# Another hand-written order of 1489 tasks for a fused long convolution and state-space scan

## The chip, the core and the metric

The kernel runs on one core of one Trainium2 chip. The metric is the device time of one execution in microseconds (us). The core has five instruction queues that run in parallel, each in its own order: TensorE (PE in the profile, its weight loads PEld), VectorE (DVE), ScalarE (ACT), GpSimd (POOL) and SyncE (SP). In this kernel SP and POOL do little but issue DMA transfers: SP's go through the queue that the profile calls q1, POOL's through q0.

## The reference, cut to what matters

Two layers work on sequences of 2048 steps and 1024 channels, and their outputs stand side by side:

```
# A: short causal filter of k, gate with v, long convolution over time, gate with q
k_shift = sum over t in 0..3 of k_pad[:, t:t+S, :] * shift_k[:, 3-t]
kv  = k_shift * v
y   = irfft(rfft(kv, 2S) * rfft(ssm_k, 2S))[:S] + kv * ssm_D
a   = q * y
# B: complex diagonal state-space layer, 1024 states
Bu  = x @ B_bar.T                     # complex
h_t = Lam_bar * h_(t-1) + Bu_t        # 2048 steps
b   = 2 * Re(h @ C.T) + x * Dskip
out = concatenate([a, b], axis=-1)
```

Tensors are bf16.

## The kernel before, in words

Both layers are cut into tasks, and one string, `ORDER`, names all 1489 of them in the order in which their instructions are issued. A word of it is `task.arguments:slots`. The letters of the slots say where a result lies: `a` is a place in `arena` (53 units of 1024 bf16 columns), `p` one of the eight PSUM banks, `h` one of three state buffers (`gslot`), `w` one of three weight slots (`wslot`). Each task goes to its own engine, every engine runs its tasks in the order of the string, and the framework sets the semaphores between them from the buffers that they read and write. So the string decides three things at once: the order on each engine's queue, which buffer must come free first, and, through the name of the task, which engine does a copy or issues a transfer.

**Layer B, sixteen chunks of 128 steps.** `bl` (L420) loads blocks of B, `bT` (L415) transposes them on PE and `bc` (L431, on ACT; `bcv` on DVE) copies them into `BT`; `cl`, `cT` and `cc`, or `cx`, do the same for C. `x.i` (L447) loads chunk i of x with a transposing DMA on SP's queue. `U.i.jp.jl` multiplies it with `BT` (L464, 16 matmuls of 128x128), `ue` (L473) copies the result out of PSUM on ACT, and `uev` does so on DVE. `r1` and `r2` (L487, L498, DVE) rotate, `cy` (L500, ACT) carries the state over, `sc` (L504, DVE) is the scan, `r3` and `r4` (L487, L510, DVE) rotate back. `yq` (L538, quarter matmuls of 64x64, eight pieces to a chunk) or `y` (L520, L523) multiplies with C, `ye` (L556) copies it out. Stores of the output are `yst` and `ysg` on POOL's queue (L563), `ysp` and `ysh` on SP's (L564).

**Layer A, two-step transforms.** `ld_w` loads the filter taps, `wb` (L402) spreads them over the partitions by a matmul with a row of ones, and `wbe` copies them out. `kp.r` (L570, and L572 with L573 for the two earlier blocks) loads blocks of k into a ring, `vp` loads v. `kvm`, `kva`, `kvb` and `kvc` (L587 to L602, DVE) build kv. `am` (L607) is the first transform, `ae` (L613) copies it out, and `ast` (L616, POOL) stores it in DRAM as `Ys_kv`; `hl`, `hd`, `hT`, `hc`, `hm`, `he` and `hst` do it for the filter, into `Ys_h`. `hd` adds `ssm_D`, on ACT, or as `hdv` on DVE.

The second transform goes over sixteen pairs. For pair i, `lw.i` (L671, SP) loads 160 KB of weights into one of the three weight slots; `lh.i` and `lk.i` (L676, SP) load 512 KB each of `Ys_h` and `Ys_kv`. For each half g = 2i, 2i+1 of the pair, `sh.g` and `sk.g` (L687, PE) transform them, and `she` (L696) and `ske` (L703) copy the results out. Two `sw.i` copies (L707) swap even and odd rows by DMA, one for each half of the rows, on POOL's queue (`sw`) or on SP's (`swp`). `pr.i` (L713, DVE) multiplies, `sa.g` (L725, PE) transforms back, `sae` (L733) copies out, `vst.i` (L736, POOL) stores 512 KB in `Vs`. The weight slot is free when the pair's last `sa` is done.

The last stage loads `vl` (L741) and q (`qp`, L746) on SP, `a3` (L753, PE) is the last transform, `a3e` (L760) copies out, `qm` (L762, DVE) multiplies with q, and `ost` (L763, POOL) or `osp` (L764, SP) stores.

A copy out of PSUM has the name of its task for ACT (`she`, `ske`, `sae`, `a3e`, `ue`, `ye`), and the name with a `v` behind it for DVE.

Setting up: `ld_par` loads five rows of parameters (L273, SP), `par_T` (L279) transposes them on PE, and `p32` (L284) copies the result out on DVE; tables are made from them.

Of the kernel before, what the change touches and what calls it, by code (L numbers as in the profile page):

```python
# [72 lines left out]
ue.1.0:a34 bl.3.1:a19 bc.4.0 U.0.0.0:p5 U.0.0.1 bl.7.0:a41 bT.2.1:p4 bl.6.1:a12 U.0.2.0:p0 bT.3.1:p7 bc.5.0 U.0.2.1
bT.7.0:p6 stt ue.0.0:a24 bl.7.1:a20 bc.2.0 bc.2.1 x.2:a52 bT.6.1:p2 bT.7.1:p3 cl.1.0:a15 kp.-2 bT.3.0:p4 bc.7.0 kring
bc.3.1 x.3:a21 bc.3.0 U.1.2.1:p5 bc.7.1 U.1.2.0 cl.1.1:a37 U.1.1.1:p1 bc.6.1 U.1.1.0 cl.3.1:a14 U.0.3.1:p4 ue.0.2 ue.1.2
kvm.1:a16 z2 kvm.2:a42 U.0.3.0 rta kva.1 kva.2 z1 U.0.1.0:p7 kvb.1:a39 cT.1.0:p6 U.3.0.1:p3 ue.0.3 kvb.2:a12 U.0.1.1
ue.0.1 cc.1.0 cT.3.1:p0 vp.1:a27 kvm.0:a16 cl.0.1:a48 kvb.3:a26 kva.0 kvc.3 cc.3.1 ld_Q ue.1.1 vp.0:a40 kvb.0:a36
# [5 lines left out]
ae.0.0.1 ast.0 am.1.0:p2p7 ae.1.0.1:a45 U.2.2.1 cx.6.1 r2.3:h2 ast.3 hT.0.1:p4 r1.1:a27 hT.0.6:p3 ae.1.1.0 U.2.3.1:p7
kvm.4:a14 ae.1.1.1 ue.2.2 cx.4.1 ae.1.0.0 r2.1:h0 hd.0 am.2.0:p6p5 hc.0.1:a22 U.2.3.0 ae.2.1.0 ast.1 cx.7.1 hd.1 ue.2.3
cT.2.0:p1 ae.2.0.0 hT.0.3:p2 cc.2.0 hc.0.6:a32 U.2.1.0:p7 U.2.1.1 hc.0.3:a13 hT.0.7:p0 hm.0.6.1:p4p1 hT.0.4:p6 cx.4.0
cy.1 kva.4 y.0.0.0:p3 ue.2.1 ast.2 sc.1.1 hc.0.4:a28 sc.1.0 hc.0.7:a12 y.0.0.1 hm.0.4.0:p2p6 kvb.4:a31 he.0.6.1.0:a43
he.0.4.0.1:a29 he.0.4.0.0 he.0.6.1.1 hT.0.0:p5 cx.5.0 hT.0.5:p0 vp.2:a34 y.0.0.2 hT.0.2:p1 r3.1:a45 hc.0.0:a19
hm.0.6.0:p6p2 he.0.6.0.0 hm.0.4.1:p5p4 he.0.4.1.1 he.0.4.1.0 y.0.0.3 hst.0.6.1 y.0.1.0:p6 kp.3 ye.0.0:a25 hc.0.5:a14
kvc.4 hst.0.4.1 y.0.1.1 he.0.6.0.1 r4.1 y.0.1.2 hm.0.0.1:p0p5 hc.0.2:a20 hm.0.7.0:p4p7 he.0.7.0.1:a50 y.0.1.3 r1.2:a15
hst.0.4.0 he.0.0.1.1:a48 hm.0.0.0:p2p3 hm.0.5.1:p7p5 y.1.1.0:p1 hst.0.6.0 he.0.7.0.0 kvm.6:a38 he.0.0.1.0 he.0.0.0.1  # L90
y.1.1.1 he.0.5.1.0:a23 he.0.0.0.0 hm.0.5.0:p4p2 he.0.5.1.1 he.0.5.0.1 vp.3:a26 am.4.0:p0p7 ye.0.1 he.0.5.0.0
ae.4.1.0:a29 x.4:a32 kp.4 y.1.1.2 y.1.1.3 y.1.0.0:p6 r2.2:h1 ae.4.0.0 kva.6 hm.0.7.1:p0p3 ye.1.1:a28 hst.0.7.0
hm.0.3.0:p2p5 hm.0.3.1:p7p4 y.1.0.1 kvm.5:a14 he.0.7.1.0 ysp.0 he.0.7.1.1 am.4.1:p1p0 cy.2 kvb.6:a19 kva.5 kvc.6
he.0.3.1.1:a36 y.1.0.2 he.0.3.1.0 kvb.5:a25 hst.0.0.1 he.0.3.0.0 hm.0.1.0:p3p2 hl.2.0:a44 sc.2.1 hst.0.5.1 hl.2.1
ae.4.0.1 U.4.3.1:p7 U.4.3.0 he.0.3.0.1 ae.4.1.1 he.0.1.0.1:a38 U.4.0.0:p2 kvc.5 hst.0.5.0 kvm.7:a13 hst.0.0.0 he.0.1.0.0
ue.4.3:a23 am.6.1:p4p7 ae.6.1.1:a17 am.6.0:p1p3 sc.2.0 hst.0.7.1 y.1.0.3 U.4.0.1 hst.0.3.1 ae.6.0.1 ae.6.1.0 ae.6.0.0
ye.1.0 hm.0.1.1:p3p1 hd.2 hm.0.2.1:p7p4 kva.7 he.0.1.1.0 he.0.1.1.1 hm.0.2.0:p0p6 he.0.2.0.1:a34 ast.6 he.0.2.1.1
hst.0.3.0 he.0.2.0.0 U.4.1.1:p5 U.4.1.0 hl.3.1:a40 r3.2:a48 ue.4.1 kvb.7:a31 hl.3.0 hT.1.4:p3 hc.1.4:a19 hT.1.5:p0
hT.1.6:p6 hst.0.1.1 hT.1.2:p4 he.0.2.1.0 hc.1.6:a22 U.4.2.1:p1 r4.2 hc.1.5:a33 hst.0.2.0 hc.1.2:a17 kvc.7 hst.0.2.1
hst.0.1.0 cy.3 ue.4.0 ast.4 hT.1.3:p5 am.5.1:p7p3 U.4.2.0 ue.4.2 y.2.0.0:p6 am.5.0:p2p0 sc.3.1 hT.1.7:p4 ae.5.0.1:a15  # L100
x.6:a37 lw.1:w2 hc.1.3:a18 y.2.0.1 ae.5.1.0 y.2.0.2 sc.3.0 hT.1.1:p1 hc.1.7:a35 hm.1.7.1:p4p5 y.2.1.0:p7 hd.3 ae.5.0.0
ae.5.1.1 am.7.0:p0p2 he.1.7.1.1:a25 hT.1.0:p5 y.2.1.1 hc.1.1:a14 ae.7.1.0:a38 kvm.8:a48 x.5:a36 ae.7.0.0 r3.3:a42
# [739 lines left out]
```

## Time and profile before

| what | value |
| --- | --- |
| median of the runs shown | 350.45 us (348.97 to 351.01) |
| the profiled execution | 352.94 us, of which the span from first to last instruction is 351.0 |
| mean granted clock of TensorE | 0.989 of full speed |
| busy: PE, DVE, ACT, POOL | 332.9, 326.1, 273.4, 68.0 us |
| DMA | 62880 packets, 101.09 MB, mean 288 GB/s |
| SP's queue (q1), POOL's queue (q0) | 67.39 MB, 32.95 MB |

The profile is of one execution. Its page gives busy times, the span in 40 slices, the queues, the chain of work that ended last and the costliest groups of instructions; the trace behind it can be asked for any stretch, any line and every wait. In a row of single instructions the first number is the start in us and the second how long it took; what stands in square brackets is the wait ahead of it and what ended it. A row of an issuing queue (SPq, POOL) gives the issue of a transfer, not its passing.

### The profile page before, as it was taken

The numbers are of one execution on the slowest core, as the hardware profiler recorded it, in microseconds if no ns is written. First come the engines' busy times: TensorE is split into PE (matmuls) and PEld (weight loads), VectorE is DVE, ScalarE is ACT, GpSimd is POOL, SyncE is SP. The second block draws the span as 40 slices with busy tenths as digits, with TensorE's granted clock in tenths as the row PEclk, the third lists the DMA queues.
The fourth block names the chain that finished last, engine by engine and source line by source line (L and its number), as shares of the span: only waits on it lengthen the run. The fifth ranks groups of instructions, "written<-read, shape, count | busy, mean of one in ns | idle before, by whom it ended". The sixth has DMA issues, their size and how long they took to land. (4 is left out here: it accounts for less than half of the span.)

```text
span 351.0 us, 11815 instructions
## 1 busy us (share of the span) xinstructions
PE 332.9 (95%) x5105; PEld 233.2 (66%) x5105; DVE 326.1 (93%) x261; ACT 273.4 (78%) x524; POOL 68.0 (19%) x110
## 2 busy tenths in 40 slices
PE   5989999999999999999999989999699999999991
PEld 2789888547856886689665565765575887754440
DVE  4999999999999999999999989999779999999961
ACT  6999999999999973798889769999378974235640
POOL 6000011343422552120111210031021122000020
PEclk9999999999999999999999999999899999999997
DMA  5999999898996888968998999898978898798996
GB/s 193 357 286 293 278 264 324 271 288 329 279 327 211 319 283 234 324 233 307 308 244 293 194 357 357 309 236 250 292 264 301 288 314 310 229 381 273 366 326 226
DMA packets 62880, 101.09 MB, mean 288 GB/s; under 512 B 29422, under 2 KB 31742, under 8 KB 62828
## 3 DMA queue, kind: packets, MB, share of 16 engines
q1 hardware_dynamic: 53228, 67.39, 66.1%
q0 software_dynamic: 9600, 32.95, 25.9%
q8 instruction: 40, 0.66, 0.8%
q14 instruction: 12, 0.10, 0.1%
HBM read 52.08 MB, written 33.55 MB: 244 GB/s over the span
## 5 line engine op out<-in xcount | busy, mean ns | idle before, releaser
L464 PEld LDWEIGHTS <-BT 128*128 128x128 bf16 x2048 | 118.4, 99 | 13.7 <-issue 9.2
L464 PE MATMUL bank<-arena,BT 128*128 128x128 bf16 x2048 | 126.0, 221 | 0.3 <-ACT BT L431 0.3
L538 PE MATMUL bank<-CT,gslot 64*64 64x512 bf16 x1408 | 88.2, 378 | 0.1
L504 DVE TENSOR_TENSOR_SCAN gslot<-rtab,gslot 128x1040 bf16<-128x1040 f32 x32 | 72.9, 2310 | 0.7
L538 PEld LDWEIGHTS <-gslot 64*64 64x64 bf16 x1408 | 38.8, 107 | 29.4 <-issue 1.4
L473 ACT CAST arena<-bank 128x512 bf16<-128x512 f32 x61 | 37.2, 642 | 14.0 <-PE bank L464 13.0
L613 ACT CAST arena<-bank 128x512 bf16<-128x512 f32 x64 | 36.6, 658 | 8.0 <-PE bank L607 5.3
L520 PE MATMUL bank<-CT,gslot 128*128 128x512 bf16 x160 | 39.4, 379 | 0.0
L696 ACT CAST arena<-bank 128x512 bf16<-128x512 f32 x62 | 33.4, 615 | 7.3 <-PE bank L687 5.7
L713 DVE TENSOR_TENSOR arena<-arena 128x4096 bf16<-128x4096 bf16 x16 | 36.5, 2285 | 2.3 <-ACT arena L473 1.6
L487 DVE TENSOR_TENSOR arena<-gslot,Z 128x4096 bf16<-128x4096 bf16 x16 | 36.6, 2288 | 0.9 <-PE bank L687 0.4
L703 ACT CAST arena<-bank 128x512 bf16<-128x512 f32 x60 | 33.7, 609 | 4.0 <-PE bank L687 2.6
L487 DVE TENSOR_TENSOR arena<-arena,Z 128x4096 bf16<-128x4096 bf16 x16 | 36.5, 2283 | 0.0
L733 ACT CAST arena<-bank 128x512 bf16<-128x512 f32 x60 | 32.7, 615 | 4.4 <-PE bank L725 4.4
L664 ACT CAST arena<-bank 128x512 bf16<-128x512 f32 x64 | 34.6, 635 | 1.7 <-PE bank L656 1.6
L587 DVE TENSOR_TENSOR arena<-arena 128x4096 bf16<-128x4096 bf16 (+3 forms) x16 | 29.9, 1880 | 0.0
L667 POOL DMA_DIRECT2D Ys_h<-arena x32 | 23.5, 737 | 28.6 <-ACT arena L664 26.1
L616 POOL DMA_DIRECT2D Ys_kv<-arena x16 | 11.1, 711 | 87.2 <-ACT arena L613 86.1
L687 PE MATMUL bank<-arena,wslot 64*64 64x512 bf16 x256 | 22.1, 383 | 4.7 <-DMA wslot<-a_c_W 4.7
L556 ACT CAST arena<-bank 128x512 bf16<-128x512 f32 x31 | 18.3, 601 | 9.9 <-PE bank L523 4.4
L760 ACT CAST arena<-bank 128x512 bf16<-128x512 f32 x26 | 13.6, 600 | 15.6 <-PE bank L753 15.6
L520 PEld LDWEIGHTS <-gslot 128*128 128x128 bf16 x160 | 14.4, 98 | 16.1 <-issue 1.5
(104 smaller groups left out, 416.8 us busy)
## 6 DMA issues: line engine op xcount, KB each, us to landing
Ys_kv<-arena POOLq DMA_DIRECT2D x16, 512.0 KB, 5.0
Ys_h<-arena POOLq DMA_DIRECT2D x32, 256.0 KB, 4.7
arena<-Ys_h SPq DMA_DIRECT2D x16, 512.0 KB, 7.2
arena<-Ys_kv SPq DMA_DIRECT2D x16, 512.0 KB, 5.4
Vs<-arena POOLq DMA_DIRECT2D x16, 512.0 KB, 5.7
arena<-Vs SPq DMA_DIRECT2D x16, 512.0 KB, 7.5
arena<-in_A_k_dram SPq DMA_DIRECT2D x8, 512.0 KB, 6.3
arena<-in_A_v_dram SPq DMA_DIRECT2D x8, 512.0 KB, 4.7
```

The source lines that it names most:

```text
L464: nc.tensor.matmul(pu[:, w, jl, :], BT[:, 2 * jp + jl, w, d, :], xT[:, d, :], start=(d == 0), stop=(d == ND - 1))
L473: cp(st["u", i][:, :, 2 * jp:2 * jp + 2, :], st.pop(("pu", i, jp)))
L487: nc.vector.tensor_mul(m, s_, win(Z))
L504: nc.vector.tensor_tensor_scan(gf, rtab[:].rearrange("p j t -> p (j t)"), gf, 0.0, ALU.mult, ALU.add)
L520: nc.tensor.matmul(py, h[:, w, j, 2:GW], CT[:, j, w, dh * 512:(dh + 1) * 512], start=(j == 0 and w == 0), stop=False)
L538: mm = nc.tensor.matmul(st["py", i, dh][cols, cs(r)], lhs(dh, rows, c), rhs(dh, rows), start=first, stop=last)
L613: cp(st["ysb", n2][:, p, dh * 512:(dh + 1) * 512], st.pop(("pa", n2, p, dh)))
L664: cp(o, st.pop(("pb", hf, s, e, r)).rearrange("p (n c t) -> p n c t", n=2, c=2))
L696: cp(st["hab", i][:, 0, a, l, :], st.pop(("ps", "h", g, l)))
L703: cp(st["x16", i][:, a, l, :], st.pop(("ps", "k", g, l)))
L713: nc.vector.tensor_mul(hab, st.pop(("x16", i)).rearrange("p a l d -> p (a l d)").unsqueeze(1).to_broadcast([P, 2, 2 * D]), hab)
L733: cp(st["vsb", i][:, a, dh * 512:(dh + 1) * 512], st.pop(("pv", g, dh)))
```

## The change

Only the text of `ORDER` differs. The 1489 tasks are the same but for the variants that name an engine or a queue. Of the copies out of PSUM, DVE does 23 instead of 20 and ACT three fewer (L760: 9 instead of 6; `shev` 4 instead of 2, `yev` 2 instead of 1, `saev` 3 instead of 4, `skev` 3 instead of 4, `uev` 2 instead of 3); `hd.0` becomes `hdv.0`. Some row swaps and some output stores change queues, so that SP's order has 138 rows instead of 136. Nearly every line of the string is another one; the lines that the prediction speaks of are these:

```diff
 ORDER = """
-ld_w:a15 wb.0:p2 ld_par wbe.0:a8 par_T:p7 p32 exp1 bl.6.0:a13 dve2 dve3 bl.0.0:a0 bl.0.1:a32 bl.1.0:a22 wb.4:p0
...
-bT.0.1:p2 sin0 bc.0.0 kp.1:a0 wb.1:p6 tabA1:a46a49a42a44 wb.6:p7 bc.0.1 wb.5:p3 kp.0 bT.1.0:p1 wbe.1 bl.5.1:a23 sin1
...
-bT.5.1:p6 bc.1.0 x.0:a38 bl.3.0:a48 bcv.6.0 eo kvm.3:a29 kp.-1 bT.1.1:p5 bT.4.0:p0 bcv.1.1 bcv.4.1 bc.5.1 kva.3 U.1.0.1
...
-yq.6.0:p7p6 ye.5.0:a11 vst.1 lk.2:a21 sh.5:p4p0 cy.7 sae.6.1 ye.5.1 yq.6.1 sh.4:p2p1 sae.6.0 she.4.1:a32 yq.6.2 yq.6.3
-she.4.0 sc.7.0 she.5.1 sk.5:p0p5 sc.7.1 r3.7:a45 sa.0:p1p3 r4.7 lh.4:a50 she.5.0 sa.1:p4p2 ske.5.1:a4 ske.5.0
...
-ske.11.1:a4 sae.5.0:a44 sk.10:p4p6 yq.7.4 yq.7.5 lk.4:a28 yq.7.6 lk.6:a21 lh.7:a12 swp.5.0 ske.10.1 sa.4:p3p6 x.11:a14
...
-yq.8.0:p1p0 yq.8.1 lw.6:w2 sh.13:p3p6 yq.8.2 lh.8:a37 lh.11:a1 sh.12:p2p5 r1.9:a40 she.13.0:a27 she.13.1 vst.2 lw.8:w1
...
-yq.10.0:p0p2 yq.10.1 ye.9.1 pr.9 sk.23:p3p4 yst.7 yq.10.2 ske.23.1 ske.23.0 sa.15:p5p1 yq.10.3 x.12:a52 sa.14:p7p3
-lw.10:w0 sae.15.1:a24 sae.15.0 sae.14.0 sa.18:p6p1 sa.19:p5p4 cy.11:h0 yq.10.4 ld_G sae.19.1:a49 sae.18.0 sw.11.0
...
-ye.10.0:a42 ye.10.1 shev.21.0:a5 she.20.1 lw.15:w2 lh.12:a1 she.21.1 U.12.1.0 sw.11.1 pr.11 ue.12.1:a22 sc.11.0
...
+ld_w:a41 wb.6:p6 wb.2:p5 wb.1:p0 wbe.1:a8 wbe.2 kp.0:a0 ld_par par_T:p1 wb.3:p7 wb.7:p4 p32 wb.0:p5 wbe.7 dd bl.2.1:a40
...
+bc.1.1 bT.0.1:p2 sin2 kva.1 bT.4.1:p0 bl.7.0:a40 kp.1 bT.5.0:p1 bc.4.1 bl.6.0:a39 bl.5.1:a43 bT.7.0:p7 x.0:a29 kp.-2
...
+bc.0.0 bc.5.1 U.1.1.0:p2 eo U.1.0.0 ue.1.0:a41 kvm.3:a35 cl.1.0:a19 U.0.2.1:p4 U.0.2.0 kvm.2:a13 U.1.2.0:p1 bc.6.0
...
+U.8.3.0:p4 r4.6 U.8.3.1 sae.3.0 cy.7 ye.5.1 pr.0 sa.7:p6p5 ue.8.3 sa.6:p1p0 sae.7.0:a38 sa.1:p3p7 vst.1 sa.0:p2p4
+sae.7.1 lh.4:a23 yq.6.0:p5p6 lh.2:a49 yq.6.1 sc.7.0 sae.1.1:a25 sae.6.0 sae.1.0 lw.2:w2 sae.0.1 lh.5:a32 r1.8:a42
...
+lk.7:a42 yq.7.5 ske.9.0 sa.11:p3p7 vst.3 r3.8:a36 sa.10:p6p0 sae.11.0:a12 sae.11.1 ske.9.1 sw.4.1 lw.6:w2 sae.10.0
...
+ske.12.1 x.11:a19 U.10.1.1 lw.8:w0 ue.10.1 lk.8:a25 sh.16:p0p3 ske.13.1 yq.8.4 ld_G swp.6.0 sk.17:p7p2 lw.7:w1
...
+she.18.1 x.12:a31 lh.12:a50 she.19.1 r2.10 sc.10.0 sc.10.1 r3.10:a7 r4.10 yst.8 sk.18:p2p4 pr.7 U.11.1.1:p6 U.11.1.0
...
+ske.22.1 lk.12:a6 sae.19.1:a33 sc.11.1 r3.11:a39 sae.18.0 U.12.0.1:p5 lw.10:w1 sh.20:p6p0 ye.10.0:a49 sae.19.0 lk.15:a8
...
+U.12.1.1 ske.21.1 vst.7 cy.12:h0 ske.20.1 uev.12.1 sa.22:p0p7 ue.12.2 sa.23:p2p6 sae.22.1:a38 sae.23.1 sae.23.0 lw.15:w2
+saev.22.0 sh.30:p3p5 shev.30.1:a44 r1.12:a34 sk.30:p1p4 x.13:a10 ske.30.0:a24 yq.11.0:p7p0 yq.11.1 sh.31:p1p2 skev.30.1
...
```

The place of `sa.0` and `sa.1` (PE) against `yq.6.0` is seen in these lines: before, eight PE tasks from `yq.6.0` to `sa.0` stand ahead of `sa.1`; now `sa.7`, `sa.6`, `sa.1` and `sa.0` stand ahead of `yq.6.0`. At three other places the queues read as follows.

SP's queue around the weight slot of pair 6 (in both pieces the L671 row that fills `wslot2`). L447 is the transposing load `x.11`, L676 the 512 KB loads, L707 the swaps, L671 the weight slots. Before:

```order
L676 DMA arena_95<-Ys_h_87 128x2x1024
L707 DMA arena_95<-arena_95 64x2048
L447 DMA_TRANSPOSE arena_95<-in_B_x_dram 128x8x128
L676 DMA arena_95<-Ys_h_87 128x2x1024
L707 DMA arena_95<-arena_95 64x2048
L671 DMA wslot2_94<-a_c_W3 128x640
L676 DMA arena_95<-Ys_h_87 128x2x1024 x2
L671 DMA wslot1_93<-a_c_W3 128x640
```

Now:

```order
L707 DMA arena_95<-arena_95 64x2048 x3
L676 DMA arena_95<-Ys_kv_86 128x2x1024
L671 DMA wslot2_94<-a_c_W3 128x640
L676 DMA arena_95<-Ys_kv_86 128x2x1024
L676 DMA arena_95<-Ys_h_87 128x2x1024 x2
L447 DMA_TRANSPOSE arena_95<-in_B_x_dram 128x8x128
L671 DMA wslot0_92<-a_c_W3 128x640
```

The slot of pair 6 was three transfers behind `x.11` and is now four ahead of it; what follows `x.11` directly now is the slot of pair 8.

SP's queue around the weight slots of pairs 10 and 15. Before, `x.12` (the L447 row), then the slot of pair 10, then that of pair 15:

```order
L671 DMA wslot1_93<-a_c_W3 128x640
L676 DMA arena_95<-Ys_h_87 128x2x1024 x3
L447 DMA_TRANSPOSE arena_95<-in_B_x_dram 128x8x128
L671 DMA wslot0_92<-a_c_W3 128x640
L671 DMA wslot2_94<-a_c_W3 128x640
L676 DMA arena_95<-Ys_h_87 128x2x1024
```

Now, from `x.12` to `x.13`; the slots of pairs 10 and 15 are the two L671 rows:

```order
L447 DMA_TRANSPOSE arena_95<-in_B_x_dram 128x8x128
L676 DMA arena_95<-Ys_h_87 128x2x1024
L676 DMA arena_95<-Ys_kv_86 128x2x1024 x2
L707 DMA arena_95<-arena_95 64x2048
L676 DMA arena_95<-Ys_h_87 128x2x1024
L707 DMA arena_95<-arena_95 64x2048
L676 DMA arena_95<-Ys_kv_86 128x2x1024
L671 DMA wslot1_93<-a_c_W3 128x640
L676 DMA arena_95<-Ys_kv_86 128x2x1024
L676 DMA arena_95<-Ys_h_87 128x2x1024
L671 DMA wslot2_94<-a_c_W3 128x640
L447 DMA_TRANSPOSE arena_95<-in_B_x_dram 128x8x128
```

Seven transfers stand now between `x.12` and the slot of pair 10, and `x.13` comes behind both slots.

The start of PE's queue: L402 are the `wb` matmuls that spread the filter taps, L279 is `par_T`. Before:

```order
L402 LDWEIGHTS ones_68
L402 MATMUL bank2_98<-arena_95,ones_68 128x512
L279 LDWEIGHTS praw_108
L279 MATMUL bank7_103<-ident_61,praw_108 128x40
L402 LDWEIGHTS ones_68
L402 MATMUL bank0_96<-arena_95,ones_68 128x512
```

Now:

```order
L402 LDWEIGHTS ones_68
L402 MATMUL bank6_102<-arena_95,ones_68 128x512
L402 LDWEIGHTS ones_68
L402 MATMUL bank5_101<-arena_95,ones_68 128x512
L402 LDWEIGHTS ones_68
L402 MATMUL bank0_96<-arena_95,ones_68 128x512
L279 LDWEIGHTS praw_113
L279 MATMUL bank1_97<-ident_61,praw_113 128x40
```

The parameter transpose came after one `wb` and comes now after three; on SP's queue its five loads stand now behind one 512 KB block of k (`kp.0`).

More of the change, by code (lines that the diff above doesn't have):

```diff
@@ L73 @@
[L73 to L77, printed above, removed]
@@ L83 @@
[L83 to L87, printed above, removed]
@@ L88 @@
[L88 to L102, printed above, removed]
@@ new lines @@
+r2.2 am.6.1:p0p4 ae.5.0.0 ae.6.1.0:a22 y.1.1.1 y.1.1.2 ae.6.0.1 kvm.7:a13 sc.2.0 hl.2.0:a44 kva.7 ae.6.1.1 sc.2.1
+kvb.7:a28 ue.4.3:a24 r3.2:a13 hm.0.1.1:p6p1 hl.2.1 hst.0.4.0 ae.6.0.0 hst.0.4.1 he.0.1.1.0:a38 hm.0.0.1:p2p0
+hm.0.0.0:p6p7 he.0.1.1.1 he.0.0.0.1:a48 y.1.1.3 hl.3.0:a40 hl.3.1 U.4.1.0:p4 U.4.1.1 he.0.0.1.0 ye.1.1 hst.0.1.1
+hm.0.1.0:p1p2 he.0.0.1.1 he.0.0.0.0 U.4.2.1:p6 ue.4.1 he.0.1.0.0 am.4.0:p0p5 ae.4.1.0:a30 ae.4.0.0 hd.2 ast.6 kvc.7
+U.4.0.1:p3 hst.0.0.1 U.4.2.0 hd.3 he.0.1.0.1 kp.4 ue.4.2 hT.1.3:p1 hc.1.3:a51 U.4.0.0 hst.0.0.0 hT.1.0:p7 hT.1.5:p0
```

185 lines of the change are left out of this document (102 added, 83 removed).

## The prediction

> **What bounds the kernel now.** I read the page first, then busy time over long stretches, then who waited for what, and then short windows around the longest waits.
>
> The page gives each engine's busy time, its share of the span and its instructions.
>
> ```profile
> PE 332.9 (95%) x5105; PEld 233.2 (66%) x5105; DVE 326.1 (93%) x261; ACT 273.4 (78%) x524; POOL 68.0 (19%) x110
> ```
>
> Two engines are nearly full, so 18 us on TensorE (PE) and 25 us on VectorE (DVE) are all that an order can win. Where most of it lies is seen in two long stretches (length, then busy us of each engine, granted clock, DMA share, GB/s):
>
> ```profile
> 45.00:180.00 135.00, 135.00 (x1966) 97.09 (x1967) 134.89 (x98) 117.54 (x228) 37.79 (x54) 1.00 0.91 282
> 180.00:260.00 80.00, 75.12 (x1420) 48.85 (x1412) 74.43 (x39) 64.61 (x132) 13.39 (x22) 0.98 0.97 282
> ```
>
> From 45 to 180 us neither engine has a gap: whatever makes either late there is still late at 180. From 180 to 260 both lose 5 to 6 us. The waits name the cause (total, times, longest):
>
> ```profile
> PE bank L687 <- DMA wslot<-a_c_W: 4.7, 3, 3.2
> DVE arena L696 <- PE bank L687: 2.5, 1, 2.5
> DVE arena L473 <- PE bank L464: 2.1, 1, 2.1
> DVE arena L713 <- ACT arena L473: 1.6, 1, 1.6
> ```
>
> PE waits for one kind of load, the 160 KB weight slots of the second transform; DVE's 2.5 and 2.1 are waits for that PE. Here are the two places, PE first, then the queues that issued what it waited for:
>
> ```profile
> 210.41 0.41 PE L687 MATMUL bank<-arena,wslot 64*64 64x512 bf16 x4 [1.32 <-DMA wslot<-a_c_W]
> 250.74 0.63 PE L687 MATMUL bank<-arena,wslot 64*64 64x512 bf16 x8 [3.19 <-DMA wslot<-a_c_W]
> ...
> 193.41 1.98 SPq L447 DMA_TRANSPOSE arena<-in_B_x_dram  x1
> 198.83 0.34 SPq L671 DMA_DIRECT2D wslot<-a_c_W  x1
> 240.78 1.27 SPq L447 DMA_TRANSPOSE arena<-in_B_x_dram  x1
> 243.02 1.32 SPq L671 DMA_DIRECT2D wslot<-a_c_W  x2
> ...
> 193.15 0.53 POOL L707 DMA_DIRECT2D arena<-arena  x1 [6.72 <-ACT gslot L500]
> 193.68 0.56 POOL L563 DMA_DIRECT2D out_dram<-arena  x1
> 241.45 0.56 POOL L563 DMA_DIRECT2D out_dram<-arena  x1 [3.08 <-ACT arena L556]
> 242.00 0.53 POOL L707 DMA_DIRECT2D arena<-arena  x1
> ```
>
> A weight slot issued at 198.83 is used at 210.41, and one issued at 243.02 at 250.74. Both stand behind a transposing load of x (L447) on SP's queue, and within 1.3 us of each of these loads POOL's queue issued at least two transfers. The two queues then nearly stop:
>
> ```profile
> 190.00:193.00 3.00, 3.00 (x76) 1.65 (x64) 2.74 (x2) 2.68 (x7) 0.00 (x0) 1.00 1.04 395
> 198.00:200.00 2.00, 1.88 (x43) 0.90 (x36) 2.00 (x2) 0.00 (x0) 0.00 (x0) 1.00 0.38 36
> 246.00:248.00 2.00, 1.55 (x36) 0.90 (x28) 1.90 (x2) 0.96 (x3) 0.00 (x0) 1.00 0.99 112
> ```
>
> The rate falls from 395 GB/s to 36 and 112. For contrast, the load issued at 227.90 has no POOL issue until 233.87, and the weight slot behind it (230.33) caused no wait above:
>
> ```profile
> 227.90 1.30 SPq L447 DMA_TRANSPOSE arena<-in_B_x_dram  x1
> 230.33 0.86 SPq L671 DMA_DIRECT2D wslot<-a_c_W  x1
> 233.87 0.73 POOL L736 DMA_DIRECT2D Vs<-arena  x1 [8.43 <-ACT arena L696]
> ```
>
> So my reading is that a transposing load that passes while POOL's transfers pass holds everything behind it on SP for about 5 us.
>
> **The change, part by part.** All sums are against the profiled execution, 352.94 us with a span of 351.0; the median of the runs shown is 350.45, or 2.5 less, and I carry the difference over unchanged.
>
> *The two holes.* In the new SP order the first slot load stands four entries ahead of the transposing load instead of three behind it. At the second place seven entries, two of them swaps that wait for late work, stand between the transposing load and the slot that followed it directly, and the next transposing load comes after both slots instead of before them. That takes PE's waits of 1.32 and 3.19, and the slow clock behind the second:
>
> ```profile
> 205.20 1.96 PE L464 MATMUL bank<-arena,BT 128*128 128x128 bf16 x32
> 251.30 3.58 PE L464 MATMUL bank<-arena,BT 128*128 128x128 bf16 x32
> 252.00:255.00 3.00, 3.00 (x32) 2.77 (x33) 3.00 (x2) 0.57 (x3) 0.00 (x0) 0.54 0.86 315
> ```
>
> The same 32 matmuls take 1.96 us at full clock and 3.58 after the wait, when the granted clock is 0.54: 1.62. Together 1.32 + 3.19 + 1.62 = 6.1 us on PE; on DVE 2.5 + 2.1 + 1.6 = 6.2.
>
> Would the new positions make holes of their own? Behind the first transposing load now stands the slot of pair 8, with 8.9 us of PE work between its release and its first use, more than the 7.7 that the slot at 243.02 took through a hole. Behind the slot of pair 15, the transposing load is followed, by the PE work between, about 3 us later by two 512 KB stores of `Vs` on POOL. If that meeting costs the same 5 us, it delays the swaps of pair 10 and one 512 KB load, wanted more than 8 us later; the next slot (pair 12) is issued some 9 us of PE work later. So nothing for either in the sum; if a cover fails it costs one hole, 3.19 + 1.62 = 4.8.
>
> *PE is now held to DVE at one place.* In the old order PE does four pieces `yq.6.0` to `yq.6.3`, `sh.5`, `sh.4`, `sk.5` and `sa.0` before `sa.1`; the new order puts `sa.1` ahead of all eight, and what DVE does ahead of `pr.0` is the same but for the small terms below. `sa.0` and `sa.1` read what `pr.0` writes.
>
> ```profile
> 179.56 2.29 DVE L713 TENSOR_TENSOR arena<-arena 128x4096 bf16<-128x4096 bf16 x1
> 180.41 0.84 PE L538 MATMUL bank<-CT,gslot 64*64 64x512 bf16 x12
> 184.76 1.06 PE L725 MATMUL bank<-arena,wslot 64*64 64x512 bf16 x16
> ```
>
> The first of the eight began at 180.41, so PE arrives at `sa.1` at 180.4 now, while `pr.0` (the DVE row) ended at 179.56 + 2.29 = 181.85. That is a wait of 1.4 us, plus whatever DVE itself is late. From the rows of the start:
>
> ```profile
> 3.67 0.58 PE L402 MATMUL bank<-arena,ones 1*128 1x512 bf16 x1 [3.67 <-DMA arena<-in_A_shift_k_dram]
> 4.18 0.21 PE L279 MATMUL bank<-ident,praw 40*128 40x40 bf16 x1
> 4.33 1.88 PE L402 MATMUL bank<-arena,ones 1*128 1x512 bf16 x4
> 4.43 0.20 DVE L284 CAST p<-bank 128x40 f32<-128x40 bf16 x1 [3.43 <-PE bank L279]
> ```
>
> DVE's first real work waits for the parameter transpose (L279), which stood behind one broadcast matmul and now stands behind three, at a pitch of (1.88 - 0.58) / 3 = 0.43: it starts at 3.67 + 3 x 0.43 = 4.96 instead of 4.18, so DVE is 0.78 late. The five parameter loads also stand behind a 512 KB load now; they have until 4.9 to land, so I add nothing (at worst one such load's time, 512 KB at 395 GB/s = 1.3 us). PE's wait at `sa.1` comes to 1.4 + 0.8 = 2.2 us. It is paid once: later places where PE now follows `pr` closely find it already that late. Bounds: 0 if PE arrives late by small waits of its own, 3.5 with the 1.3.
>
> *Copies between engines.* Evictions done by DVE go from 20 to 23, and one tiny add moves from ScalarE to DVE.
>
> ```profile
> L760 DVE CAST arena<-bank 128x512 bf16<-128x512 f32 x6 | 4.0, 687 | 0.5 <-PE bank L753 0.4
> ```
>
> Three at 0.687 make 2.1 us of DVE; the add (no row; DVE's small operations are near 0.2) is below the rounding. ScalarE, 78% busy, gains nothing by losing them.
>
> *Tighter loads.* Two later weight slots have 4.5 and 4.2 us of PE work between the release of their slot and their first use, and the `Vs` load that the last stage needs first is now fourth in its burst. What such a slot takes:
>
> ```profile
> wslot<-a_c_W SPq DMA_DIRECT2D x16, 160.0 KB, 3.3
> DMA to landing us min/median/max: 3.3/5.7/8.1
> ```
>
> (the first row is the whole run's median, the second the seven slots issued from 190 to 252, holes included). At 3.3 they fit, at 5.7 they cost 1.2 and 1.5. I take 1.0 in all, bounds 0 and 3.
>
> *The end* keeps its shape: last matmuls, one eviction, one store by each queue; 0.
>
> The sum on PE: -6.1 + 2.2 + 1.0 = -2.9. On DVE: -6.2 + 0.8 + 2.1 = -3.3, with some of the 1.0 on top. Both engines end within a microsecond of each other, so I take -3.0: 349.9 for the profiled execution, 347.4 for the median.
>
> [...]
>
> **The rivals.**
>
> *Full gain.* PE is late enough by itself at `sa.1` and all loads fit: DVE's -3.3 is the floor of that part, and the wait near the end goes too:
>
> ```profile
> DVE arena L762 <- DMA arena<-in_A_q_dram: 2.8, 1, 2.8
> ```
>
> In the new order the last loads of q have 7 us or more of work to land in. -3.3 - 2.8 = -6.1: 344.3. Against it: this asks every tight place to hold.
>
> *A hole moves.* The meeting named above, or one of another load, delays something wanted at once; one hole of 4.8 comes back: 347.4 + 4.8 = 352.2, or 350 where half is covered. For it: five transposing loads must still pass among POOL's stores. I put it at 351.
>
> *The holes are not made by the meeting.* If the stalls come from the mere number of transfers in flight, they return wherever the queues are as full: nothing won, 2.2 + 1.0 lost, 350.45 + 3.2 = 353.7, slower. For it: SP's queue was eight transfers deep at both. Against: the undisturbed load at 227.90. [...]
>
> *DVE loses at the start.* Its product `kvm.3` needs a block of k (`kp.1`), now behind fifteen other loads instead of eight.
>
> ```profile
> 0.00:10.00 10.00, 5.97 (x26) 2.48 (x27) 5.01 (x16) 6.97 (x12) 5.63 (x17) 1.00 0.68 195
> 10.00:20.00 10.00, 9.49 (x124) 9.16 (x124) 9.62 (x25) 9.90 (x24) 0.00 (x0) 1.00 1.08 362
> ```
>
> With itself these are three blocks of 512 KB and thirteen of 256 KB, 5.0 MB; 1.95 MB pass in the first 10 us and the rest at 362 GB/s in 8.4, so it lands near 18.4. DVE reaches it near 20.7 us (5.2, and some 15.5 of work ahead by the groups' means). Each microsecond beyond that is one lost, as 45 to 180 shows no slack; from 24 on the gain is gone, and at 27 the time is 350.45 + 3.3 = 353.7. Against it: the pace would have to fall by a third or more.
>
> **How the numbers follow.** Chances: forecast 0.50 (own range 345.5 to 349), full gain 0.14, a hole moves 0.16, not the meeting 0.12, late start 0.08. A measurement here tells no change from about 0.5%, which is 1.75 us: below 348.7 is faster, above 352.2 slower. Faster: nine tenths of the forecast and the full gain, 0.45 + 0.14 = 0.59. Slower: a fifth of the moved hole and the last two, 0.03 + 0.12 + 0.07 = 0.22. The same: 0.19. The range, 344.0 to 353.0, runs from the full gain to most of the moved hole and leaves out about 1 in 10 at each end.
>
> **What would show it.** Right: no wait of L687 for a weight slot above 1 us, the granted clock at full from 200 to 330, no window under 120 GB/s while slot loads wait, a PE wait near 2 us at 180 to 183 at L725, DVE's first copy near 5.2. Wrong: holes with no transposing load in them (the meeting is then not the cause), a wait of DVE at L587 before 25 us, or many small PE waits for ScalarE's evictions, whose cost I put at nothing because ScalarE is 78% busy.

## The result: 0.6% slower by the ratio, against a forecast of 0.9% faster

| | median of the executions shown | lowest to highest | profiled execution, its span |
| --- | --- | --- | --- |
| before | 350.62 us (20) | 347.00 to 353.26 | 352.94, 351.0 |
| changed | 351.35 us (20) | 350.12 to 353.66 | 353.08, 351.3 |

The ratio of changed to before is 1.0056, with a 95% interval of 1.0033 to 1.0080. It leaves out executions more than 1.5% above the fastest of their kernel, which takes four of the twenty from the kernel before and none from the changed one, so it is larger than the quotient of these medians, 1.002. The forecast was 347.4 with a range of 344.0 to 353.0: the time lies inside the range, but the gain of 3 us is not there; by the ratio the change loses 2.0 us, by the medians 0.7.

The page of the changed kernel, its first part:

```profile
PE 330.2 (94%) x5085; PEld 234.4 (67%) x5105; DVE 327.7 (93%) x265; ACT 272.4 (78%) x519; POOL 70.1 (20%) x113
```

DVE is busy 1.6 us longer than before (326.1); the rest is nearly the same. The long stretches tell more (length, then busy us of PE, PEld, DVE, ACT and POOL, granted clock, DMA share, GB/s). The changed kernel:

```profile
0.00:20.00 20.00, 12.42 (x105) 8.55 (x105) 13.03 (x31) 14.28 (x21) 5.11 (x16) 1.00 0.90 267
20.00:45.00 25.00, 23.58 (x407) 22.84 (x406) 24.76 (x41) 25.00 (x45) 0.00 (x0) 1.00 1.16 291
45.00:180.00 135.00, 133.13 (x1913) 95.83 (x1926) 134.64 (x98) 116.94 (x222) 38.66 (x56) 1.00 0.89 276
180.00:260.00 80.00, 79.25 (x1537) 55.50 (x1537) 77.41 (x43) 70.29 (x143) 13.31 (x21) 1.00 0.97 301
260.00:300.00 40.00, 38.05 (x694) 28.63 (x687) 34.45 (x25) 27.55 (x55) 7.95 (x12) 1.00 0.87 293
```

and the kernel before, where the prediction had not shown them:

```profile
0.00:20.00 20.00, 15.46 (x148) 11.64 (x149) 14.64 (x39) 16.86 (x35) 5.63 (x17) 1.00 0.88 279
20.00:45.00 25.00, 24.03 (x403) 22.65 (x401) 25.00 (x34) 25.00 (x35) 0.00 (x0) 1.00 1.17 289
260.00:300.00 40.00, 40.00 (x746) 30.41 (x743) 37.12 (x26) 29.58 (x60) 7.55 (x11) 1.00 0.84 296
```

From 180 to 260 us PE is now busy 79.25 instead of 75.12, and the clock is full: the two holes are gone, as forecast. But by 45 us PE has done 36.0 us of work instead of 39.5, and DVE 37.8 instead of 39.6; from 45 to 180 PE idles 1.87 us where it had no gap; and from 260 to 300 DVE idles 5.55 us instead of 2.88. The waits behind that (total, times, longest), the changed kernel again:

```profile
DVE p L284 <- PE bank L279: 5.7, 1, 5.7
PE bank L402 <- DMA arena<-in_A_shift_k_dram: 5.1, 1, 5.1
DVE arena L713 <- DMA arena<-arena: 4.5, 2, 3.1
DVE arena L556 <- PE bank L538: 1.5, 1, 1.5
```

No wait for a weight slot (`wslot`) is left. In its place DVE waits twice for row swaps (L707, `arena<-arena`), 3.1 us of it ahead of `pr.13`, and everything starts later. The single instructions at the start, PE and DVE of the changed kernel:

```profile
5.10 1.43 PE L402 MATMUL bank<-arena,ones 1*128 1x512 bf16 x3 [5.10 <-DMA arena<-in_A_shift_k_dram]
6.71 0.20 DVE L284 CAST p<-bank 128x40 f32<-128x40 bf16 x1 [5.71 <-PE bank L279]
```

PE's first matmul, which needs the filter taps, comes at 5.10 instead of 3.67, and DVE's first copy at 6.71 instead of 4.43. And around 280 us, SP's queue, POOL's queue, and then DVE:

```profile
279.99 4.41 SPq L746 DMA_DIRECT2D arena<-in_A_q_dram  x5
281.27 1.11 POOL L707 DMA_DIRECT2D arena<-arena  x2 [1.01 <-ACT arena L696]
290.86 2.29 DVE L713 TENSOR_TENSOR arena<-arena 128x4096 bf16<-128x4096 bf16 x1 [3.13 <-DMA arena<-arena]
```

SP issues five 512 KB loads of q at 280 to 284 us; POOL issues both swaps of pair 13 in the middle of them, and these land at 290.7, 9 us later.

### The profile page after: what moved, and what is told of

The parts are those of the page before. It is cut to its first block, busy times and chain, and to the rows that moved or that the text cites. A ratio compares the mean times of both kernels' runs of the same rounds, so it can differ in the third digit from the quotient of the medians.

```text
span 351.3 us, 11805 instructions
## 1 busy us (share of the span) xinstructions
PE 330.2 (94%) x5085; PEld 234.4 (67%) x5105; DVE 327.7 (93%) x265; ACT 272.4 (78%) x519; POOL 70.1 (20%) x113
## 5 line engine op out<-in xcount | busy, mean ns | idle before, releaser
L464 PEld LDWEIGHTS <-BT 128*128 128x128 bf16 x2048 | 116.5, 98 | 15.4 <-issue 9.4
L464 PE MATMUL bank<-arena,BT 128*128 128x128 bf16 x2048 | 124.2, 219 | 1.9 <-ACT BT L431 1.4
L538 PEld LDWEIGHTS <-gslot 64*64 64x64 bf16 x1408 | 41.5, 107 | 26.2 <-issue 1.3
L473 ACT CAST arena<-bank 128x512 bf16<-128x512 f32 x62 | 37.9, 627 | 15.6 <-PE bank L464 14.0
L713 DVE TENSOR_TENSOR arena<-arena 128x4096 bf16<-128x4096 bf16 x16 | 36.4, 2282 | 4.5 <-DMA arena<-arena 4.5
L520 PE MATMUL bank<-CT,gslot 128*128 128x512 bf16 x152 | 38.6, 380 | 0.9 <-DVE arena L760 0.2
L703 ACT CAST arena<-bank 128x512 bf16<-128x512 f32 x61 | 34.3, 615 | 6.6 <-PE bank L687 5.6
L733 ACT CAST arena<-bank 128x512 bf16<-128x512 f32 x61 | 33.2, 604 | 6.8 <-PE bank L725 6.7
L613 ACT CAST arena<-bank 128x512 bf16<-128x512 f32 x64 | 36.1, 644 | 2.5 <-PE bank L607 1.4
L664 ACT CAST arena<-bank 128x512 bf16<-128x512 f32 x64 | 34.4, 614 | 4.5 <-PE bank L656 4.2
L696 ACT CAST arena<-bank 128x512 bf16<-128x512 f32 x60 | 32.7, 609 | 3.7 <-PE bank L687 3.5
L556 ACT CAST arena<-bank 128x512 bf16<-128x512 f32 x30 | 18.0, 613 | 15.8 <-PE bank L538 9.3
L587 DVE TENSOR_TENSOR arena<-arena 128x4096 bf16<-128x4096 bf16 (+3 forms) x16 | 30.0, 1882 | 0.0
L736 POOL DMA_DIRECT2D Vs<-arena x16 | 11.8, 738 | 50.4 <-ACT arena L733 33.9
```

Of the source, the lines that this page charges most:

```text
L464: nc.tensor.matmul(pu[:, w, jl, :], BT[:, 2 * jp + jl, w, d, :], xT[:, d, :], start=(d == 0), stop=(d == ND - 1))
L473: cp(st["u", i][:, :, 2 * jp:2 * jp + 2, :], st.pop(("pu", i, jp)))
L520: nc.tensor.matmul(py, h[:, w, j, 2:GW], CT[:, j, w, dh * 512:(dh + 1) * 512], start=(j == 0 and w == 0), stop=False)
L538: mm = nc.tensor.matmul(st["py", i, dh][cols, cs(r)], lhs(dh, rows, c), rhs(dh, rows), start=first, stop=last)
L613: cp(st["ysb", n2][:, p, dh * 512:(dh + 1) * 512], st.pop(("pa", n2, p, dh)))
L664: cp(o, st.pop(("pb", hf, s, e, r)).rearrange("p (n c t) -> p n c t", n=2, c=2))
```

## The experiments

The kernels below were timed on four chips, and the kernel before again on each: 350.93, 350.79, 350.08 and 351.36 us. Where a difference is small, kernels timed on one chip are compared; where the two were on different chips, the text says so.

### The kernel before, profiled a second time

> The kernel before, unchanged, looked at a second time. Theory 1 (the two holes belong to the order): a second profile shows PE waiting for a weight slot again, at sh.13 about 1.3 us and at sh.21 about 3.2 us, and a slow clock behind the second. Theory 2 (the profiled execution was an unlucky one, 2.3 us above the median): the two waits sum to 2 us or less, and no window of slow clock follows.

It measured 350.26 us (350.93 for the other executions of the kernel before on that chip). The profiled execution took 349.19 us, 3.8 less than the first. Its waits, and its row at `sh.21`:

```profile
PE bank L687 <- DMA wslot<-a_c_W: 3.1, 1, 3.1
DVE arena L696 <- PE bank L687: 2.7, 1, 2.7
249.08 0.63 PE L687 MATMUL bank<-arena,wslot 64*64 64x512 bf16 x8 [3.05 <-DMA wslot<-a_c_W]
250.00:255.00 5.00, 5.00 (x89) 4.48 (x87) 4.96 (x4) 4.20 (x9) 0.58 (x2) 1.00 0.82 300
```

One wait of 3.05 us is there again; the wait of 1.32 at `sh.13` is not, and the clock behind the hole is full. Theory 1 holds for the second hole. Theory 2 holds for the first: of the two further profiles below that leave `x.11` at its old place (`yst.9` and `sw.11.1` moved; the start alone), neither shows that wait.

For the slow clock one profile can't decide, but the mean granted clock was taken of every execution: 0.989 in the first profile, which has the slow stretch, and 0.994 in this one, which hasn't. Of 116 executions of the kernel before on the four chips, 81 have a mean of 0.991 or less, with a median of 351.27 us, and 35 have 0.992 or more, with 348.62. So the first profile shows the usual kind and the second the rarer one, as far as the means tell: what belonged to the first execution alone is the wait of 1.32.

### The holes alone

```diff
-x.11:a14 ... lw.6:w2
+lw.6:w2 x.11:a14
-x.13:a31 ... x.12:a52 sa.14:p7p3 lw.10:w0 ... x.15:a0
+x.13:a31 x.12:a0 ... sa.14:p7p3 lw.10:w0 ... x.15:a37
```

> The kernel before with only the two meetings taken out: the transposing load x.11 is issued behind the weight slot of pair 6 instead of ahead of it, and x.12 is loaded some 12 us earlier, right behind x.13, into a place that is free by then (x.15 takes another free place in turn). Theory 1: both waits of L687 for a weight slot vanish and the time falls by 5 to 6 us. Theory 2 (typical executions hold little of these holes): it falls by 0 to 2.5 us. Rival (the stalls come from the number of transfers in flight): the waits stay and nothing is won.

346.19 us, ratio to before 0.9898 (0.9863 to 0.9932); the unchanged kernel took 350.26 and 350.93 on the same chip, 4.1 and 4.7 us more. Three stretches of this run:

```profile
0.00:20.00 20.00, 13.62 (x112) 10.06 (x113) 12.79 (x35) 16.88 (x35) 5.63 (x17) 1.00 0.90 255
20.00:45.00 25.00, 24.33 (x418) 23.39 (x416) 25.00 (x36) 24.28 (x33) 0.00 (x0) 1.00 1.17 284
180.00:260.00 80.00, 79.35 (x1556) 52.31 (x1551) 78.49 (x45) 69.79 (x142) 15.59 (x25) 1.00 0.96 307
```

The holes are worth 3.6 us by the ratio and 4.1 or 4.7 by the medians: between the two theories' numbers, and not the 6.1 of the forecast. No execution of this run has a mean clock below 0.993, so the slow clock went with the holes; beside the executions of the unchanged kernel with 0.991 or less on that chip (33 of 46, median 351.47) the gain is 5.3, beside the others (348.27) it is 2.1. A second fact is in the rows: without the holes PE has only 0.67 and 0.65 us of gaps in the last two stretches. So what PE loses in the first 20 us should be paid at the end, even with a wait of DVE near it (2.4 us for q in this run) left as it is; the section on the start tests that.

### What makes the second hole

```diff
-yst.9 ... lw.15:w2 ... sw.11.1              # both by POOL
+lw.15:w2 swp.11.1 ... lk.12:a39 ysp.9   # both by SP, behind the slots
```

> The kernel before with x.12 and the weight slot of pair 10 left where they are on SP's queue; only POOL's two transfers that pass at the same time are taken away: the output store yst.9 and the swap sw.11.1 are issued by SP, behind the weight slots of pairs 10 and 15. Theory 1 (the stall is made by the meeting with POOL's transfers): the slot lands about 5 us after its issue instead of 7.7, PE's wait of 3.1 us ahead of sh.21 falls below 1, and the time falls by 2 to 3 us. Rival (the stall is made by the transposing load ahead of the slot, or by the number of transfers on SP's queue): the wait stays at 3 us and the time stays.

348.25 us, ratio 0.9933 (0.9891 to 0.9974). The rows at `sh.21`, the matmuls and their weight loads:

```profile
248.04 0.63 PE L687 MATMUL bank<-arena,wslot 64*64 64x512 bf16 x8 [0.66 <-ACT arena L556]
248.04 0.14 PEld L687 LDWEIGHTS <-wslot 64*64 64x64 bf16 x8 [0.96 <-DMA wslot<-a_c_W]
```

PE's wait falls from 3.05 to 0.66. The profile puts that down to ScalarE, but the weight loads of the same matmuls waited 0.96 for the slot, which landed only at 248.00; so a small part of the hole is left. No execution of this run has a mean clock below 0.992. With the two runs above there are three of the four combinations, by the issues and landings in the traces:

| `x.12` ahead of the slot | POOL's two transfers beside it | slot of pair 10, issue to landing | POOL's two transfers |
| --- | --- | --- | --- |
| yes | yes (unchanged, second profile) | 241.64 to 249.04: 7.4 us | 8.0 and 8.2 us |
| yes | no (this run) | 242.98 to 248.00: 5.0 us | issued by SP, later |
| no | yes (holes alone) | 243.68 to 246.81: 3.1 us | 3.7 us each |

The profile's rows for POOL's two transfers (KB of one, us to landing), unchanged kernel first, then the kernel without the holes:

```profile
out_dram<-arena POOLq DMA_DIRECT2D x1, 256.0 KB, 8.0
arena<-arena POOLq DMA_DIRECT2D x1, 256.0 KB, 8.2
...
out_dram<-arena POOLq DMA_DIRECT2D x1, 256.0 KB, 3.7
arena<-arena POOLq DMA_DIRECT2D x1, 256.0 KB, 3.7
```

Neither partner alone makes 7.4, and both queues suffer when they meet: POOL's transfers take twice as long. So the meeting is the cause of most of the hole, as the prediction read it, and a count of transfers on SP's queue, the rival, is not: what stood ahead of the slot there was the same with and without POOL's two. The transposing load alone costs something too, 5.0 against 3.1. Each row is one profiled execution, and the fourth combination, neither partner, was not run. How the hardware makes the two hold each other up is not shown by these runs. The Trainium skill ("DMA: Bandwidth & Descriptors", section "Rules for kernel authors") says that "A transpose next to ordinary DMAs needs nothing". That row is about silent corruption when two transposing streams overlap; it says nothing of time, and no run here tests it.

### The start

Into the kernel before I put what marks the changed kernel's start, two blocks of k early and the parameter transpose late:

```diff
-ld_w:a15 wb.0:p2 ld_par ... par_T:p7 ... bl.0.1:a32 ... kp.1:a0 ... kp.0
+ld_w:a15 wb.0:p2 kp.1:a0 ld_par ... wb.4:p0 wb.7:p1 par_T:p7 ... bl.0.1:a32 kp.0
```

(with `bl.0.0` at a free place, since the ring of k begins earlier).

> The kernel before with the changed kernel's start put into it: one block of k (512 KB) ahead of the parameter loads, a second one behind three loads of B, and the parameter transpose behind three broadcast matmuls. Theory 1 (PE is dense from 45 us to the end, so what PE loses in the first 20 us is paid at the end): first broadcast matmul at 5.1 instead of 3.6, PE's busy time in the first 20 us down by 2 us or more, and the time up by 2 to 3 us. Rival (the start has slack): within 0.8 us.

355.33 us, ratio 1.0153 (1.0101 to 1.0206): more than theory 1 had. The profile says why: the hole was larger in it, and the granted clock behind it, from 253 to 258 us, was 0.50.

```profile
PE bank L687 <- DMA wslot<-a_c_W: 5.2, 1, 5.2
```

So the same start went into the kernel without holes.

> The kernel before without the two meetings (346.2 us), and with the changed kernel's start put into it: one block of k ahead of the parameter loads, a second one behind three loads of B, the parameter transpose behind three broadcast matmuls. It measures the start without the hole, which had grown from 3.1 to 5.2 us in the run that had the start alone. Theory 1 (PE is dense from 45 us on): what PE loses by 45 us, 2 to 3 us, is in the time: 348.2 to 349.2. Rival (most of that run's loss was the larger hole): 346.2 to 347.

348.71 us, 2.5 more than without this start, on another chip; the kernel before, timed on both, was 0.4 slower on that one (351.36 against 350.93), which leaves 2.1. By the ratios to the kernel before (0.9918 against 0.9898) it would be only 0.7. The traces lie with the larger number: the spans are 348.6 and 346.3, and the rows by 45 us are

```profile
0.00:20.00 20.00, 12.29 (x85) 8.76 (x86) 11.73 (x34) 14.92 (x30) 5.63 (x17) 1.00 0.90 274
20.00:45.00 25.00, 24.10 (x416) 23.47 (x415) 23.93 (x34) 24.59 (x37) 0.00 (x0) 1.00 1.14 272
```

36.4 us of PE work instead of 37.95, and 35.7 of DVE work instead of 37.8: 1.6 and 2.1 lost. I take the start at about 2 us, and no better than to a microsecond: with the old start PE's work by 45 us is anything from 37.95 to 39.5 in the profiles shown here.

Undoing it in the changed kernel was less simple. First only the parameters:

```diff
-wb.6:p6 wb.2:p5 wb.1:p0 wbe.1:a8 wbe.2 kp.0:a0 ld_par par_T:p1
+wb.6:p6 ld_par par_T:p1 wb.2:p5 wb.1:p0 wbe.1:a8 wbe.2 kp.0:a0
```

> The changed kernel with only the start put back: the five parameter loads ahead of the first block of k on SP's queue, and the parameter transpose behind one broadcast matmul instead of three. DVE's first copy should come at 4.4 us again instead of 6.7. Theory 1 (DVE has no slack to the end): the time falls by 2.3 us. Rival (PE or later waits take the gain back): 0 to 0.8 us.

351.25 us (351.35 before the edit, in the runs of the result): nothing, the rival's number. DVE did start early, and PE gave it back (waits of this run):

```profile
DVE p L284 <- PE bank L279: 3.4, 1, 3.4
PE bank L415 <- DMA arena<-in_B_B_re_dram: 2.3, 1, 2.3
```

PE now waits 2.3 us for a block of B that stands behind 512 KB of k. The start is set by the order of the loads, not by the instruction that is first ready. So the next run leaves the parameters first and moves k behind the first six loads of B and `x.1`:

```diff
-... bl.2.0:a22 kp.-1 bl.1.1:a14 ... x.1:a33 wbe.6
+... bl.2.0:a22 bl.1.1:a14 ... x.1:a33 kp.0 kp.-1 wbe.6
```

> The changed kernel with the parameter loads first, the parameter transpose behind one broadcast matmul, and the first two blocks of k (kp.0 and kp.-1, 1 MB) behind six loads of B and x.1 instead of among them. Theory 1 (loads of B behind k are what starves PE in the first 20 us; moving the parameters alone did not help because k stayed ahead of B): PE's busy time in the first 20 us rises from 12.4 to 14 or more, DVE waits for k about 1 us ahead of kvm.1, and the time falls by 1.5 to 2.5 us. Rival (DVE's product of k is what must start early): DVE waits 2 us or more for k and nothing is won.

350.04 us, 1.3 less than the changed kernel's 351.35 (on another chip). PE's first stretch is 13.63 us instead of 12.42, less than the 14 expected; the gain is a little below theory 1's range. The rival (DVE starved for k by 2 us or more) isn't seen: DVE's first product of k waits 1.1 us, and by the profile for PE.

### The swaps

> The changed kernel, unchanged, looked at a second time: which of its waits belong to the order and which to one execution. Theory 1: DVE waits for the swaps again ahead of pr.9 and pr.13 (1.4 and 3.2 us in the first look, 1.6 and 1.2 in the run with another start) and for PE ahead of yev.11.0 (1.6). Rival: the 3.2 was that execution's, and 1.2 is the rule.

350.92 us, where the kernel before took 351.36 on the same chip: ratio 1.0029 (0.9992 to 1.0065). So two chips don't settle whether the changed order is slower at all; that it gains no 3 us they do. The second profile of the changed kernel (execution of 351.90):

```profile
DVE arena L713 <- DMA arena<-arena: 2.9, 2, 1.5
DVE arena L556 <- PE bank L538: 1.5, 1, 1.5
```

The two waits for swaps are there again, with 2.9 us in all instead of 4.5: the order makes them, and for the size the rival is right: none is longer than 1.5, so the 3.1 ahead of `pr.13` was that execution's.

```diff
-... sw.14.0 ... sw.13.1 ... swp.14.1 ... sw.13.0 ... qp.7:a2 ... qp.0:a15
+... sw.14.0 ... swp.14.1 swp.13.1 ... swp.13.0 ... qp.7:a2 ... qp.0:a15
```

> The changed kernel with only the two row swaps of pair 13 moved from POOL's queue to SP's, ahead of the five loads of q that are issued at 280 to 284 us. Theory 1 (the 2.5 MB of q hold the swaps up): the swaps land within 5 us, DVE's wait of 3.1 us ahead of pr.13 is gone, and the time falls by about 3 us. Rival (the path goes on through another wait directly behind): 1 us or less.

349.74 us, 1.5 less than the edit of the start on the same chip (351.25), which had changed nothing. SP issues the swaps ahead of the loads of q, and DVE runs through three products without a wait:

```profile
279.18 3.11 SPq L707 DMA_DIRECT2D arena<-arena  x3
282.39 2.73 SPq L746 DMA_DIRECT2D arena<-in_A_q_dram  x5
283.00 6.69 DVE L713 TENSOR_TENSOR arena<-arena 128x4096 bf16<-128x4096 bf16 x3
```

The mechanism is theory 1's. The size is half of it, about what the second profile gives for the longer wait (1.5).

```diff
-x.12:a31 lh.12:a50 ... lk.10:a35 ... lk.11:a41 ... lh.10:a22 ... lk.15:a8
+x.12:a31 lk.11:a41 ... lh.10:a22 lk.10:a35 ... lk.15:a8 lh.12:a50
```

> The changed kernel with the swaps of pair 13 ahead of the loads of q, as in the run before, and with three 512 KB loads on SP's queue reordered so that the swap of pair 9 and the load wanted at 243 us (lk.11) stand ahead of lk.10 and lh.12, which are wanted at 254 and 264. Theory 1 (DVE's wait of 1.4 us ahead of pr.9 comes from these loads): that wait is gone, and the time falls by another 1.4 us, to about 348.3. Rival (PE is the bound there): another 0.5 us or less.

349.00 us, with the swaps of pair 13 moved as well. Both waits for swaps are gone from DVE's list. The further gain is 0.7 us between chips, and lies between the two theories.

### All three edits, and DVE's extra copies

> The changed kernel with three edits together: k behind the loads of B at the start (1.3 us by itself), the swaps of pair 13 ahead of the loads of q (1.6 by itself), and lk.10 and lh.12 behind the swap of pair 9 (0.7 on top of that). Theory 1 (each is a separate delay of the same nearly full engines): they add up to 3.6, 347.7 us. Rival (they overlap, the later ones being covered once PE or DVE is earlier): 348.8 or more.

348.56 us, the rival's side: the three singly gave 1.3 + 1.6 + 0.7 = 3.6, each beside a kernel on another chip, together 2.8 of the changed kernel's 351.35.

```diff
-saev.22.0 ... skev.31.0 ... yev.11.0:a14
+sae.22.0 ... ske.31.0 ... ye.11.0:a14
```

> As the run before it, and in addition three of DVE's copies out of PSUM go back to ScalarE (yev.11.0, saev.22.0, skev.31.0), which gives DVE as many copies as it had before the change. Theory 1 (DVE is a bound, so its copies cost what they take, and yev.11.0 a wait of 1.6 us beside): 2.1 us or more below that run. Rival (PE is dense there and sets the end): within 0.5 us of it.

351.36 us, 2.8 more than the run before it, on the same chip: the opposite of theory 1, and outside the rival too. DVE's longest waits from 240 to 300 us, first with DVE's copies, then with them on ScalarE:

```profile
DVE arena L556 <- PE bank L538: 1.5, 1, 1.5
```

```profile
DVE arena L733 <- ACT arena L696: 5.4, 1, 5.4
DVE arena L696 <- ACT arena L696: 1.2, 1, 1.2
```

PE waits for ScalarE at two places. At the first, ScalarE has four copies of `sa.22` and `sa.23` in a row instead of three, and `yq.11` waits for the last of them. At the second, `ye.11.0` waits 1.92 us for PE's last piece of `yq.11`; the copy behind it (`she.24.1`) waits with it, and PE for that one (ScalarE's and PE's rows):

```profile
257.33 2.05 ACT L733 CAST arena<-bank 128x512 bf16<-128x512 f32 x4 [1.32 <-PE bank L725]
259.44 0.84 PE L538 MATMUL bank<-CT,gslot 64*64 64x512 bf16 x11 [1.06 <-ACT arena L733]
268.19 0.58 ACT L556 CAST arena<-bank 128x512 bf16<-128x512 f32 x1 [1.92 <-PE bank L538]
268.68 0.59 ACT L696 CAST arena<-bank 128x512 bf16<-128x512 f32 x1
269.32 0.41 PE L687 MATMUL bank<-arena,wslot 64*64 64x512 bf16 x4 [1.18 <-ACT arena L696]
```

The edit put each copy on ScalarE at the place where it had stood in the string, and at these places PE's matmuls wait for it or for the copy behind it on ScalarE's queue. The two waits, 1.06 and 1.18, make most of the 2.8 us. So that is the price of the positions, not of ScalarE's load: an engine that is busy 78% of the span can be the last one at a place. What the third copy costs isn't seen.

### A kernel that is faster than both

```diff
 (the kernel without the two meetings, and)
-... bl.5.0:a20 ld_F x.1:a33 exp2 bl.2.0:a14
+... bl.5.0:a20 ld_F bl.2.0:a14 x.1:a33 exp2
```

> The kernel before without the two meetings (346.2 us), and with one load of B (bl.2.0) ahead of the transposing load x.1 on SP's queue instead of behind it, since PE waited 1.8 to 2.4 us for that block at 10 to 12 us. Theory 1 (PE dense from 45 us on, so an earlier start is won in full): 345 us. Rival (DVE's first products then set the start): 346.2.

345.61 us, against 350.08 for the kernel before on that chip: ratio 0.9893 (0.9845 to 0.9941). That is 0.6 below the kernel without holes, on another chip and in six executions, so what this edit adds isn't shown. PE's wait of 2.36 us for that block is gone, and PE's first stretch is 15.21 us instead of 13.62; but the first profile of the kernel before has 15.46 there with the load in its old place. From 45 us on PE has no long wait:

```profile
45.00:180.00 135.00, 135.00 (x1965) 97.18 (x1966) 134.71 (x98) 117.51 (x228) 37.75 (x54) 1.00 0.92 282
260.00:300.00 40.00, 40.00 (x752) 30.44 (x748) 39.21 (x26) 25.11 (x51) 6.08 (x9) 1.00 0.81 281
```

## Why the prediction was wrong, step by step

- **What bounds the kernel** (PE and DVE full, little to win but the two places): right. The kernel without the meetings shows PE as the one that decides.
- **The meeting of a transposing load with POOL's transfers**: right as a cause of the second hole (7.4, 5.0 and 3.1 us in three combinations). One of its proofs was weak: I took low rates, 36 and 112 GB/s, as the mark of a meeting. The load at 227.90 that met nothing shows a low rate too, in the same trace:

```profile
230.00:232.00 2.00, 2.00 (x52) 1.43 (x41) 2.00 (x1) 2.00 (x5) 0.00 (x0) 1.00 0.82 55
```

  In the run without POOL's two transfers the rate is 109 GB/s from 245 to 247 us, and in the changed kernel 102 from 210 to 212, behind `x.11`, without a wait of PE. A transposing load passes slowly in these traces in any case; the meeting makes it, and what is behind it, last longer.
- **The two holes, -6.1**: this term is the step that failed first. They are worth 3.6 to 4.7. The execution that I read took 352.94, and I carried its 2.5 us above the median over unchanged, while I took its waits whole. Of these the 3.19 came again (3.05); the slow clock, 1.62, is the usual case but not every execution's (81 of 116 by the mean clock); the 1.32 of the first hole is in none of the three further profiles with `x.11` at its place. So I counted as a gain what a typical execution loses only in part.
- **PE held to DVE at `sa.1`, +2.2**: the size was nearly that of the true loss, the place was not. PE's and DVE's rows there in the changed kernel:

```profile
183.64 1.92 PE L725 MATMUL bank<-arena,wslot 64*64 64x512 bf16 x32
181.82 2.28 DVE L713 TENSOR_TENSOR arena<-arena 128x4096 bf16<-128x4096 bf16 x1
```

  `pr.0` ends at 184.10, and PE, in the four `sa` from 183.64 on without a wait, reaches `sa.1` later than that. PE was late already, which was the lower bound that I had written (0). The loss is at the start: DVE 2.28 us later instead of 0.78. The two matmuls more are 0.85 of it, close to the 0.78. The rest is the early 512 KB load, whose effect I had left at nothing, with 1.3 as the worst, and had looked for in the wrong place: it isn't the parameters behind it on SP's queue that come too late, but the filter taps on POOL's, and with them PE's first matmul, 1.43 us later; the parameter transpose runs at 6.47, right behind the three matmuls ahead of it. With the early load behind the parameters (the first edit of the changed kernel's start) PE's first matmul is back at 3.66. That a loss of 2 us at the start is nearly the 2.2 of the sum is luck.
- **Many small waits of PE for ScalarE**, which the prediction put at nothing and named as a sign of being wrong: they are there. Those of the changed kernel up to 45 us:

```profile
PE bank L464 <- ACT BT L431: 1.4, 2, 1.2
PE bank L415 <- ACT arena L408: 1.1, 1, 1.1
PE bank L415 <- ACT BT L431: 0.8, 1, 0.8
```

  They sum to 3.3 us, against 1.0 in the kernel before, and to 2.0 in the second profile of the changed kernel. They are part of what PE loses by 45 us; no run takes them apart from the late loads.
- **Tighter loads, +1.0**: the wrong ones. The weight slots of pairs 12 and 13 and the first `Vs` load cause no wait in the list. Instead two pairs of row swaps land late behind bulk loads; in the first profile they cost 4.5 us of DVE, in the second 2.9, and putting them ahead of those loads won 1.5 and 0.7. The sum had no term for them. I had named the swaps of pair 10 as covered, and had not asked of the other swaps what stood ahead of them on the other queue.
- **Copies between engines, +2.1 on DVE**: DVE's busy time rose by 1.6, but "ScalarE gains nothing" was wrong at the places of these copies: the three put back on ScalarE there cost 2.8 us. What DVE's longer busy time costs by itself is not shown.
- **DVE's late start through `kp.1`** (a rival): not seen; there is no wait of L587 in the changed kernel. Its neighbour mattered: k stood ahead of B, and once the parameters came first PE waited 2.3 us for B.
- **The wait for q near the end** (the full-gain rival's 2.8): gone in the changed kernel, without a visible gain; with PE dense to the end, as in the kernel without holes, that wait of DVE costs little.

The sum by what was measured: -3.6 to -4.7 for the holes, about +2 for the start, +2.2 for the two pairs of swaps, together between 0.5 us faster and 0.6 slower. Measured is 0.7 slower by the medians of the result and 0.4 faster by those on the chip of the changed kernel's second profile; by the ratios it is 2.0 (1.2 to 2.8) and 1.0 slower. By the ratios about a microsecond is left that no run assigns. The three edits say that more may be: together they win back 2.8 of the 4.2 for start and swaps, and the changed kernel with them, 348.56, is still 2.4 above the kernel without holes (on another chip) and 2.9 above the fastest kernel here (on the same one). Waits of PE for ScalarE and DVE's extra copies are my guess for that, and only that.
